# A list scheduler in place of a hand-written order, in a two-layer recurrent attention kernel on one core

## The chip, the cores and the metric

One core of a Trainium2 chip runs the whole program in one launch. The metric is the device time of that launch in microseconds (us). Its engines run side by side (in before PE is busy for 77%, DVE for 43% and ACT for 34% of the span), and the program gives each of them its instructions in a fixed order: PE (TensorE) does matmuls and writes them to the memory PSUM, DVE (VectorE) and ACT (ScalarE) do everything on vectors and empty PSUM, POOL (GpSimd) does a few copies, SP issues DMA. The kernel before takes 2516.9 us, median of three runs between 2516.39 and 2517.16.

## The reference, cut to what matters

```python
def _A_ref(x, mem0, Wq, Wk, Wv, Wo, seg_len):      # H = 16 heads of 256, model width 448
    mem = mem0                                      # 8 memory rows
    for s in range(2048 // 32):                     # 64 segments of 32 rows
        h = concat([mem, x[:, s*32:(s+1)*32]])      # 40 rows
        q, k, v = h @ Wq, h @ Wk, h @ Wv            # per head
        p = softmax(where(mask, q @ k.T / 16, -1e9))
        o = (p @ v) @ Wo                            # summed over heads
        mem = o[:8]; outs.append(o[8:])             # memory rows go to the next segment
def _B_ref(x, W_gate, W_up, W_down):                # width 1792
    return (relu(x @ W_gate) * (x @ W_up)) @ W_down
x = A_x
x = x + _A_ref(layernorm(x), ...);  x = x + _B_ref(layernorm(x), ...)
x = x + _A_ref(layernorm(x), ...);  x = x + _B_ref(layernorm(x), ...)   # same weights
```

The memory rows make a recurrence: segment s+1 cannot start before the memory rows of segment s are there. All else of a segment (its 32 ordinary rows, the output product, layer norm, the B layer) may come later.

## The kernel before

Set-up computes M = Wq·Wkᵀ and N = Wv·Wo for each head, so that scores are h·M·hᵀ and the output is P·h·N. After it the kernel makes 68 steps. Step t works on segment t of the first pair of layers and on segment t-4 of the second (`LAG = 4`), so steps 4 to 63 hold two segments and the four at each end hold one. Names used below:

- T: h·M, 7 units of 32 matmuls into one of two pairs of PSUM banks (`R<-hT,Mw` in the profile), each emptied by a copy to TTm (memory queries) and one to TTs (segment queries).
- The memory recurrence: scores from TTm (`bC<-hT,TTm`), softmax, transpose, P·h (`bC<-PTm,hK`), memory U·N (`bC<-Nw,UTm`), and back into hT through `selm`.
- Segment work: scores (`bG<-hT,TTs`), softmax, transpose (`bG<-ident,Ps`), segment products P·h in four quarters (`R<-PTs,hK`), copied to the buffer U.
- Once per pair of steps: U·N, 56 matmuls (`bO<-Nw,big`), layer norm with a transpose (`bG<-ident,xn`), gate and up (`R<-xBT,big`), down (`bO<-big,hB`), and the layer norm for the pair after next.

In the hand order, work that may wait stands in a list `fill`, from which every step takes bites with fixed sizes at fixed places.

```python
    def step(self, t):
        ...
        for i, k in enumerate([6, 0, 1, 2, 3, 4, 5]):
            S.t_unit(t, k, i % 2, ("act", "dve")[i % 2])      # bank pair and engine fixed
            for _ in range(2):
                if side: side.pop(0)()                        # ln_b, segment softmax of t-1
        ...
        useg = S.u_seg_units(t - 1)
        if s == 0: S.fill = useg + (S.un_units(p - 1) if p >= 1 else [])
        else:      S.fill = S.b_units(p - 1) if p >= 1 else []; late = useg
        S.run_fill(500);  S.s_mem(t); S.s_seg(t); S.run_fill(1500)
        S.p_t_mem(t); S.run_fill(400); S.u_mem(t)
        S.seg_mask(t)                                         # scores + mask, on DVE
        ...
    def un_units(self, p):
        uk = [("U", s, l, c) for s in range(2) for l in range(2) for c in range(4)]
        for k in range(0, NO, 2):                             # each waits for all of U
            def fn(k=k):
                sc.pe([MM(S.bO[:, 0:D], S.U[:, o, :], S.N[:, o, :], ...) for o in (k, k + 1)], uk, S.ps(4))
                ...
```

A helper turns each list of keys that an operation reads and writes into semaphore waits. Layer norm uses Ln and then Exp on ACT.

## Time and profile before

The first fence shows the page of the profile of before: span, busy time of each engine, the granted PE clock in 40 slices (9 is nine tenths or more), and the chain of waits by engine.

```profile
span 2520.5 us, 67762 instructions
...
PE 1940.4 (77%) x30924; PEld 1399.6 (56%) x30924; DVE 1074.5 (43%) x2630; ACT 861.8 (34%) x1859; POOL 94.3 (4%) x160
...
PEclk9778888898898888988898889888988888889888
...
PE 59%; DVE 24%; ACT 13%; issue 4%; POOL 0%; DVEq 0%; ACTq 0%; POOLq 0%
...
```

No engine is full. The second fence is the windows view of before for four stages: set-up, the single-layer steps at the head, steps 4 to 63, and the tail. After each stretch and its length come busy times and counts by engine, the clock, DMA share and rate. I set the borders at the first T matmul of steps 0, 4 and 64, which is found by counting (224 T matmuls a step).

```profile
...
core 0: us, PE busy (x) PEld busy (x) DVE busy (x) ACT busy (x) POOL busy (x), PEclk, DMA share, GB/s
0.00:110.70 110.70, 71.90 (x644) 48.03 (x644) 71.72 (x156) 63.56 (x126) 17.38 (x21) 0.89 0.61 179
110.70:214.70 104.00, 81.11 (x1484) 55.62 (x1485) 41.54 (x125) 25.44 (x70) 7.97 (x15) 0.80 0.01 3
214.70:2366.30 2151.60, 1665.94 (x26995) 1213.75 (x26995) 916.57 (x2219) 725.76 (x1556) 66.69 (x120) 0.88 0.01 3
2366.30:2520.50 154.20, 121.47 (x1802) 82.23 (x1802) 44.67 (x130) 47.05 (x109) 2.22 (x4) 0.85 0.01 3
...
```

Steps 4 to 63 take 2151.6 us, 71.72 us for each of 30 pairs of steps. PE is idle for 2151.60 - 1665.94 = 485.7 us of it, 16.2 us per pair, and its mean clock there is 0.88. In this trace the recorded clock is only ever 1.0 or 0.5, so that mean is (1 - 0.8847) · 2 = 23% of the time, 16.5 us per pair, at half clock (called cold below, and full clock warm; 0.8847 is the mean before rounding).

PE's part of the view of waits: who waited for whom, us in total, times, the longest.

```profile
...
engine line waited for: us in total, times, longest us
PE bG L126 <- DVE xn L507: 193.8, 35, 5.7
PE R L126 <- DVE big L294: 97.7, 40, 3.4
PE bG L126 <- DVE Ps L659: 77.0, 67, 1.7
PE bO L126 <- DVE big L294: 61.2, 32, 1.9
...
```

And the timeline of before, in three of the worst places of a pair: start, duration, engine, operation, and in brackets the idle time before it and what ended it.

```profile
...
start us, us, engine line op out<-in xcount [idle before <-releaser]
...
1002.32 0.39 PE L126 MATMUL R<-PTs,hK 40*128 40x512 bf16 x2 [3.06 <-DVE big L294]
...
1019.14 0.62 PE L126 MATMUL R<-PTs,hK 40*128 40x512 bf16 x6
...
1021.68 2.42 PE L126 MATMUL bO<-Nw,big 128*128 128x448 bf16 x6 [1.92 <-DVE big L294]
...
1040.93 1.28 ACT L498 ACT_TABLE_LOAD   x1
...
1042.23 0.29 ACT L498 ACTIVATE stat<-stat,cvec 128x1 f32<-128x1 f32 x1
1042.54 1.28 ACT L500 ACT_TABLE_LOAD   x1
...
1044.81 0.61 PE L126 MATMUL bG<-ident,xn 128*128 128x128 bf16 x4 [5.73 <-DVE xn L507]
...
```

A segment product (`R<-PTs,hK`) waits 3.06 us until the copies (`big<-R`) give back its bank pair. U·N (`bO<-Nw,big`) starts 1.92 us late because it waits for the last copy of the segment products. The transposes of the second layer norm wait 5.73 us, 2.56 us of which are two loads of ACT's function tables, one for Ln and one for Exp.

### The profile page before, as it was taken

To read this page: it belongs to the slowest core of one execution; us is meant where nothing else is said; L and a number is where in the kernel's file an instruction comes from. 1 tells how busy PE (TensorE), PEld (TensorE's weight loads), DVE (VectorE), ACT (ScalarE), POOL (GpSimd) and SP (SyncE) were. 2 spreads that over 40 slices of the span, in tenths; PEclk is the share of its full clock that TensorE was granted. 3 is DMA by queue.
4 is the path that set the end of the run, shared out by engine and by line. 5 is a ranking of instruction groups with operands and counts; after the bars stand their busy time and mean duration, and the time that the engine had idled before them with its cause. 6 is when DMAs were issued, how large, how long until landed. Compare 5 with 4: busy or idle time off the path is not lost.

```text
span 2520.5 us, 67762 instructions
## 1 busy us (share of the span) xinstructions
PE 1940.4 (77%) x30924; PEld 1399.6 (56%) x30924; DVE 1074.5 (43%) x2630; ACT 861.8 (34%) x1859; POOL 94.3 (4%) x160
## 2 busy tenths in 40 slices
PE   8578777787778777777787777777877777778787
PEld 5345555555555555555565555655555556555554
DVE  8334444344444444444444444444444443444332
ACT  7322333333333333333333333333333333333332
POOL 1100000000000000000000000000000000000000
PEclk9778888898898888988898889888988888889888
DMA  7300000000000000000000000000000000000000
GB/s 205 111 3 3 2 4 4 4 3 4 3 4 3 4 4 4 3 3 3 4 3 3 4 3 4 3 4 4 3 4 3 4 4 3 3 3 3 3 3 3
DMA packets 22302, 27.53 MB, mean 11 GB/s; under 512 B 5744, under 2 KB 15744, under 8 KB 22016
## 3 DMA queue, kind: packets, MB, share of 16 engines
q1 hardware_dynamic: 22016, 23.20, 3.2%
q8 instruction: 243, 3.98, 0.7%
q14 instruction: 43, 0.35, 0.0%
HBM read 21.35 MB, written 1.84 MB: 9 GB/s over the span
## 4 chain that ended last, share of the span: by engine, by line
PE 59%; DVE 24%; ACT 13%; issue 4%; POOL 0%; DVEq 0%; ACTq 0%; POOLq 0%
PE R L126 28%; PE bO L126 21%; PE bC L126 6%; DVE big L294 5%; DVE TTs L294 4%; ACT L500 3%; PE bG L126 3%; ACT TTs L292 2%; ACT L498 2%; DVE xn L507 2%; DVE TTm L294 1%; DVE hK L294 1%; DVE hB L800 1%; DVE stat L657 1%; DVE Ps L659 1%
## 5 line engine op out<-in xcount | busy, mean ns | idle before, releaser
L126 PE MATMUL R<-hT,Mw 128*128 128x80 bf16 (+1 forms) x15232 | 653.5, 212 | 45.2 <-issue 23.1
L126 PEld LDWEIGHTS R<-hT,Mw 128*128 128x128 bf16 x15232 | 639.3, 108 | 76.2 <-issue 38.6
L126 PE MATMUL bO<-Nw,big 128*128 128x448 bf16 x1904 | 437.9, 386 | 62.5 <-DVE big L294 61.2
L126 PEld LDWEIGHTS bO<-Nw,big 128*128 128x128 bf16 x1904 | 188.0, 105 | 260.7 <-DVE big L294 67.2
L292 ACT ACTIVATE TTm<-R 128x128 bf16<-128x128 f32 (+3 forms) x272 | 73.2, 269 | 634.2 <-PE R L126 609.8
L126 PE MATMUL R<-xBT,big 128*128 128x128 bf16 x3808 | 232.7, 220 | 28.2 <-ACT TTs L292 27.5
L126 PEld LDWEIGHTS R<-xBT,big 128*128 128x128 bf16 x3808 | 215.9, 98 | 33.9 <-ACT TTs L292 31.8
L294 DVE CAST TTm<-R 128x128 bf16<-128x128 f32 (+3 forms) x272 | 75.5, 277 | 308.9 <-PE R L126 283.8
L126 PE MATMUL R<-PTs,hK 40*128 40x512 bf16 (+1 forms) x640 | 95.3, 385 | 131.4 <-DVE big L294 97.7
L126 PE MATMUL bC<-Nw,UTm 128*32 128x448 bf16 x3752 | 194.6, 359 | 1.4 <-DVE UTm L294 1.4
L126 PE MATMUL bG<-ident,xn 128*128 128x128 bf16 x272 | 39.4, 297 | 193.8 <-DVE xn L507 193.8
L294 DVE CAST TTs<-R 128x512 bf16<-128x512 f32 (+3 forms) x272 | 177.0, 651 | 0.0
L294 DVE CAST big<-R 128x512 bf16<-128x512 f32 (+1 forms) x256 | 146.9, 618 | 53.7 <-PE R L126 50.8
L292 ACT ACTIVATE big<-R 128x512 bf16<-128x512 f32 (+2 forms) x268 | 136.2, 560 | 82.9 <-PE R L126 82.9
L294 POOL COPY hK<-xn 32x448 bf16<-32x448 bf16 x136 | 75.6, 556 | 2242.0 <-DVE xn L507 2235.6
L713 DVE TENSOR_TENSOR lo<-bC,hi 128x448 bf16<-128x448 f32 x67 | 41.9, 625 | 263.7 <-ACT hi L712 258.2
L800 DVE TENSOR_TENSOR hB<-gT,R 128x512 bf16<-128x512 bf16 (+1 forms) x136 | 84.2, 619 | 163.2 <-PE R L126 159.0
L292 ACT ACTIVATE TTs<-R 128x512 bf16<-128x512 f32 (+3 forms) x272 | 153.2, 563 | 0.0
L126 PEld LDWEIGHTS bC<-Nw,UTm 128*32 128x32 bf16 x3752 | 95.6, 98 | 94.8 <-issue 29.2
L126 PEld LDWEIGHTS bG<-ident,xn 128*128 128x128 bf16 x272 | 22.7, 126 | 209.1 <-DVE xn L507 209.1
L126 PEld LDWEIGHTS R<-PTs,hK 40*128 40x128 bf16 (+1 forms) x640 | 23.6, 101 | 189.7 <-DVE big L294 128.6
L126 PE MATMUL bO<-big,hB 128*128 128x448 bf16 x476 | 95.9, 353 | 21.0 <-DVE hB L800 21.0
(125 smaller groups left out, 1797.2 us busy)
## 6 DMA issues: line engine op xcount, KB each, us to landing
big<-in_A_Wo_dram SPq DMA_DIRECT2D x4, 896.0 KB, 6.0
big<-in_A_Wq_dram SPq DMA_DIRECT2D x4, 768.0 KB, 7.8
big<-in_A_Wk_dram SPq DMA_DIRECT2D x4, 768.0 KB, 9.2
big<-in_A_Wv_dram SPq DMA_DIRECT2D x4, 768.0 KB, 5.6
XA<-in_A_x_dram SPq DMA_DIRECT2D x32, 56.0 KB, 2.1
out_dram<-ys SPq DMA_DIRECT2D x32, 56.0 KB, 1.9
big<-in_B_W_down_dram SPq DMA_DIRECT2D x1, 1568.0 KB, 15.5
big<-in_B_W_gate_dram SPq DMA_DIRECT2D x1, 1344.0 KB, 6.9
```

What stands on the lines that cost most here:

```text
L126: ins = E.matmul(out, lhsT=lhsT, rhs=rhs, **kw)
L292: self.sc.op("act", lambda E: E.activation(out, src, ACT.Copy), reads, writes)
L294: self.sc.op(eng, lambda E: E.tensor_copy(out, src), reads, writes)
L498: sc.op("act", lambda E: E.activation(st[:, so + 8:so + 9], st[:, so + 7:so + 8], ACT.Ln, bias=S.cvec[:, 0:1], scale=1.0), [(key, 1), ("cv ...
L500: sc.op("act", lambda E: E.activation(st[:, so + 9:so + 10], st[:, so + 8:so + 9], ACT.Exp, scale=-0.5), [(key, 2)], [(key, 3)])
L507: sc.op("dve", lambda E, a=a, b=b, src=src: E.tensor_scalar(S.xn[:, i, a:b], src, st[:, so + 6:so + 7], st[:, so + 9:so + 10], op0=ALU.sub ...
L657: lambda: sc.op("dve", lambda E: E.tensor_reduce(st[:, 48:48 + n], Sm, AX.X, ALU.add), [("Sm",)], [("ss", 1)]),
L659: lambda: sc.op("dve", lambda E: E.tensor_tensor(dst, Sm, bc(56), ALU.mult), [("Sm",), ("ss", 2)], [("Ps",)]),
L713: sc.op("dve", lambda E: E.tensor_tensor(S.lo[:, :], b[:, 0:D], S.hi[:, :], ALU.subtract), S.ps(6) + [("hi",)], [("lo",)])
L800: sc.op("dve", lambda E: E.tensor_tensor(S.hB[:, 4 * k:4 * k + len(fcs), :].rearrange("p a b -> p (a b)"), S.gT[:, r, 0:n], S.banks[2 * r ...
```

## The change

The change intends to let a program find the order. Every operation past the set-up becomes a node with modelled durations, the keys it reads and writes, and one or two engines that may do it. A list scheduler then repeatedly takes, among operations that could start at about the same time, the one with the longest path behind it (the longest chain of operations that still has to follow); it also picks the PSUM bank pair and, for PSUM copies, ACT or DVE. The result is still a fixed program.

```diff
+    def graph(self):
+        ...
+        for o in reversed(self.ops):
+            own = min(o.cost.values()) + self.LAT[o.eng[0]]
+            o.prio = own + max([q.prio + 60.0 for q in o.succs], default=0.0)
+    def run(self):
+        while len(order) < total:
+            for e in self.ENGS:
+                ...                                     # start time of each ready candidate on e
+                lim = max(f, t0) + (60.0 if e == "pe" else 40.0)
+                t, o = max((x for x in lst if x[0] <= lim), key=lambda x: (x[1].prio, -x[0]))
+            ...
+            if len(o.eng) > 1:                          # the engine that ends first takes a copy
+                ...
@@ scalar engine
+                    eng.add_instruction(mybir.InstLoadActFuncSet(act_func_set_id=LN_EXP, name="I-4000000"))
@@ s_seg: the mask is added by PE
+            out = [MM(b[:, 0:8 * KEYS], S.ident[:, :], S.maskr[:, :], start=True, stop=False)]
@@ un
-            def fn(k=k):
-                sc.pe([MM(S.bO[:, 0:D], S.U[:, o, :], ...) for o in (k, k + 1)], uk, S.ps(4))
+            S.mm(lambda k=k: [MM(S.bO[:, 0:D], S.U[:, o, :], ...) for o in (k, k + 1)],
+                 2 * S.pitch(D), uk, S.ps(4))           # uk as before: all of U
@@ b_layer: seven pieces instead of four, down waits piece by piece
-        for k in range(4):
+        for k in range(7):
+            fcs = (2 * k, 2 * k + 1)
+            R = S.tile("R", 2)
@@ _need: DVE and ACT also wait for their own earlier readers of what they overwrite
-                if src != eng or eng == "pool":
+                if src != eng or eng != "pe":
@@ step: no fill, no places
-        S.run_fill(500)
-        ...
+        S.s_seg(t); S.seg_pt(t); S.u_seg(t)
+        if s == 1:
+            ...
+            S.un(p); S.ln_b(p); S.b_layer(p)
+            if p + 2 < NP: S.ln_a(p + 2)
```

(Cut to its core; cuts are marked with dots.)

## The prediction

> **What bounds it now.** Three stages, seen in the windows view: set-up until the first matmul of the recurrence at 110.7 us; eight single-layer steps at the ends (104 us before 214.7, 92 us after 2428.9); between them 60 two-layer steps, 2214 us, or 73.8 us per pair of steps. The pairs decide. In a pair PE is busy 57 us, DVE 31, ACT 24.5: no engine is full; the order of the PE stream is the limit. The timeline of one pair shows PE still for 5.7 us before the transposes of the second layer norm (bG<-ident,xn), 3.1 and 1.9 us around the copies of the segment products (big<-R), and about 1 us several times around softmax and TTs copies. The chain of waits agrees: PE 59%, DVE 24%, ACT 13%.
>
> The idle stretches cost twice. [...] after the 5.7 us gap the granted clock reads 0.50, and elsewhere 32 cold T matmuls (R<-hT,Mw) take 2.3 us where warm ones take 1.3. The mean clock of a pair is 0.88.
>
> **What PE needs, from stretches with clock 1.00 (estimate).** Per pair: T 448 at 36 ns (96 in 3.60 us) 16.1; U·N 56 at 189 ns (24 in 4.70) 10.6; memory U·N twice 2.83, 5.7; gate/up 112 at 56 ns, 6.3; down 2.7; small products and transposes about 8; array-shape switches and the added mask matmul about 1.3. Together about 51 of 73.8 us.
>
> **What the change does.** Arithmetic is nearly the same. It removes the mask add on DVE (0.48 us, twice a pair; a 320-wide matmul replaces it) and the ACT table loads (136 of 1.28 us; two before each layer norm, 2.6 us of its latency). Gate/up goes in 7 pieces instead of 4 (about +0.9 us of ACT and DVE per pair). Above all it moves: U·N, the B layer and layer norms leave their fixed slots, T units may run ahead, copies choose the engine that ends first.
>
> Two loops could prevent filling. The memory recurrence: T 8.1 us, copies, softmax and transposes about 6.5, memory U·N 2.8: about 18 us per step, 36 per pair, below 51. The other, scores, U·N, layer norm, B, layer norm, to T of the pair after next, is about 35 us by its durations and has over one pair of time. So PE should bind, with leftovers where both loops wait or copies hold the two R bank pairs: I allow 4 us.
>
> **Sum.** Set-up 110; 30 pairs at 54.5, 1635; head about 85, tail about 83. About **1915 us**, 8 in 10 between **1835 and 2030**. Faster by over 2%: 0.97; within: 0.02; slower: 0.01.
>
> **What would show it.** PE busy 88 to 93% of the span, no idle over 3 us in the pairs; clock 0.97 or more; pairs of 53 to 57 us; no ACT_TABLE_LOAD past the start; "PE bG <- DVE xn" waits (194 us) almost gone; chain mainly PE. Set-up still ends at 110.
>
> **What would make it wrong.** The static order rests on modelled times; engines run in order, so one late copy stalls PE: then many waits of 0.3 to 1 us and 58 to 62 us per pair. Finer alternation of shapes could cost PE more. If the greedy order finishes the filler early, the recurrence is left alone with 5 us idle per step. [...]

110 + 1635 + 85 + 83 is 1913, about 1915 us. The smaller terms are estimates, and these measured numbers stand behind them. At full clock in before, a memory U·N matmul starts 283 ns after a U·N matmul and not 189 (33 places), so a change of array shape costs about 94 ns there; with 17 changes a pair that would make 1.6 us, more than the 1.3 estimated. The mask matmul took 136 ns (after, start to start). A copy of 512 columns took 597 ns on ACT and 688 on DVE for the gate and up products, one of 256 columns 383 and 412, which gives the 0.9 us for seven pieces. And that one late copy stalls PE is seen in before: `lo`, which the next `selm` matmuls read, was ready at 1001.15 us, but they started at 1003.15, behind the segment product that stood still for a bank until 1002.32.

## The result, and the profile after

The kernel after takes 1988.25 us (median of four fast runs, 1986.36 to 1989.57) against 2517.03 for before in the same rounds. The ratio is 0.7898, 95% interval 0.7884 to 0.7911. Here and below a ratio is the mean time of one kernel's fast runs over that of before's fast runs of the same rounds, so it is not quite the ratio of the medians quoted. The forecast was 1915 us, with a range of 1835 to 2030: the result lies in the range, 73 us above the middle.

The same lines of the page of after:

```profile
span 1986.3 us, 68251 instructions
...
PE 1825.2 (92%) x30992; PEld 1305.1 (66%) x30992; DVE 1013.9 (51%) x2529; ACT 771.0 (39%) x1960; POOL 94.3 (5%) x160
...
PEclk9869999999999999999999999999999999999999
...
PE 68%; DVE 17%; ACT 2%; issue 1%; DVEq 0%
...
```

The windows view of after for the same four stages, borders found in the same way:

```profile
...
0.00:111.30 111.30, 73.00 (x644) 49.22 (x645) 73.87 (x158) 61.79 (x127) 17.49 (x21) 0.90 0.59 178
111.30:205.10 93.80, 84.32 (x1528) 56.42 (x1529) 31.70 (x110) 29.21 (x87) 7.95 (x15) 0.87 0.01 3
205.10:1870.10 1665.00, 1564.56 (x27071) 1127.68 (x27070) 867.54 (x2132) 644.60 (x1646) 66.68 (x120) 0.96 0.02 4
1870.10:1986.30 116.20, 103.29 (x1753) 71.78 (x1752) 40.80 (x129) 35.35 (x100) 2.22 (x4) 0.94 0.01 4
...
```

A pair of steps takes 1665.0 / 30 = 55.50 us. PE idle fell from 16.2 to (1665.00 - 1564.56) / 30 = 3.35 us per pair, cold time from 16.5 to 4.2. So 12.8 of the 16.2 us that a pair lost are idle time. The rest is for the most part PE work done at a better clock: from one T matmul to the next it now takes 36.3 ns on the average where it took 42.1 (442 such distances in a pair before: 2.6 us).

PE's waits in after (total us, times, longest):

```profile
...
PE R L127 <- DVE big L710: 47.4, 61, 1.4
PE bO L127 <- DVE big L710: 25.2, 31, 0.8
...
PE bG L127 <- DVE xn L743: 7.0, 4, 3.7
...
```

The wait of 193.8 us for the layer norm has gone. What is left is for the most part one place (2.4 of the 3.35 us idle per pair), shown by the timeline of after:

```profile
...
966.86 1.96 DVE L710 CAST big<-R 128x512 bf16<-128x512 f32 x3
...
967.70 0.39 PE L127 MATMUL R<-PTs,hK 40*128 40x512 bf16 x2 [1.38 <-DVE big L710]
...
968.74 0.23 DVE L826 TENSOR_REDUCE stat<-bC 128x2 f32<-128x80 f32 x1
...
969.45 3.14 PE L127 MATMUL bO<-Nw,big 128*128 128x448 bf16 x8 [0.84 <-DVE big L710]
...
```

The segment products (`R<-PTs,hK`) of the second step of a pair stand still 1.38 us for a bank pair, then U·N 0.84 us for the last copy. DVE works without a pause here (`big<-R`, three copies in 1.96 us), and the memory softmax, which would give PE other work, begins behind those copies (968.74). The windows view of after, one microsecond each, with the clock as the third number from the end:

```profile
...
966.00:967.00 1.00, 0.32 (x4) 0.00 (x0) 0.94 (x3) 0.85 (x2) 0.00 (x0) 1.00 0.00 0
967.00:968.00 1.00, 0.30 (x2) 0.12 (x2) 1.00 (x2) 0.23 (x1) 0.00 (x0) 1.00 0.00 0
968.00:969.00 1.00, 0.40 (x6) 0.14 (x4) 1.00 (x4) 0.87 (x2) 0.00 (x0) 1.00 0.24 57
969.00:970.00 1.00, 0.55 (x2) 0.28 (x3) 0.97 (x3) 0.30 (x2) 0.00 (x0) 0.73 0.00 0
970.00:971.00 1.00, 1.00 (x4) 0.40 (x3) 0.76 (x6) 0.50 (x2) 0.00 (x0) 0.50 0.00 0
...
973.00:974.00 1.00, 1.00 (x15) 0.41 (x13) 0.00 (x0) 0.01 (x1) 0.73 (x2) 1.00 0.00 0
...
```

Just after that place the clock halves, with no single idle gap above 1.38 us: PE was busy for 0.30 to 0.55 us of each microsecond. The first 8 matmuls of U·N then take 3.14 us, about twice their warm time (1.69 us for 8 in before, at 1031.12 us). The whole trace shows the same: all changes of the clock lie on a grid of 3.413 us, and in steps 4 to 63 PE was busy for 29 to 53% of the 30 full-clock stretches of this grid after which the clock halved, and for 74 to 100% of the 418 after which it stayed full. In before the two ranges overlap (0 to 65%, and 49 to 100%), so the busy share alone does not settle it.

### The profile page after: what moved, and what is told of

It is laid out like the page before. It is cut to its first block, busy times and chain, and to the rows that moved or that the text cites. A ratio compares the mean times of both kernels' runs of the same rounds, so it can differ in the third digit from the quotient of the medians.

```text
span 1986.3 us, 68251 instructions
## 1 busy us (share of the span) xinstructions
PE 1825.2 (92%) x30992; PEld 1305.1 (66%) x30992; DVE 1013.9 (51%) x2529; ACT 771.0 (39%) x1960; POOL 94.3 (5%) x160
## 4 chain that ended last, share of the span: by engine, by line
PE 68%; DVE 17%; ACT 2%; issue 1%; DVEq 0%
PE R L127 35%; PE bO L127 22%; PE bC L127 8%; DVE big L710 7%; PE bG L127 2%; DVE stat L736 1%; DVE ys L1007 1%; DVE xn L743 1%; DVE XA L1003 1%; DVE hK L710 1%; DVE UTm L710 1%; DVE XB L978 1%; DVE Ps L870 1%; DVE hB L996 1%; DVE stat L868 1%
## 5 line engine op out<-in xcount | busy, mean ns | idle before, releaser
L127 PE MATMUL R<-hT,Mw 128*128 128x80 bf16 (+1 forms) x15232 | 548.7, 200 | 23.9 <-POOL hT L710 22.9
L127 PEld LDWEIGHTS R<-hT,Mw 128*128 128x128 bf16 x15232 | 539.7, 100 | 39.0 <-issue 24.0
L127 PE MATMUL bO<-Nw,big 128*128 128x448 bf16 x1904 | 463.5, 388 | 25.2 <-DVE big L710 25.2
L127 PE MATMUL R<-xBT,big 128*128 128x128 bf16 x3808 | 251.7, 220 | 22.9 <-DVE xBT L710 22.2
L996 DVE TENSOR_TENSOR hB<-gT,R 128x256 bf16<-128x256 bf16 x238 | 100.0, 420 | 325.4 <-ACT gT L995 322.4
L127 PEld LDWEIGHTS R<-xBT,big 128*128 128x128 bf16 x3808 | 224.6, 98 | 46.2 <-DVE xBT L710 27.7
L995 ACT ACTIVATE gT<-R 128x256 bf16<-128x256 f32 x238 | 91.2, 383 | 183.4 <-PE R L127 179.5
L709 ACT ACTIVATE big<-R 128x512 bf16<-128x512 f32 (+1 forms) x263 | 134.6, 543 | 63.3 <-PE R L127 61.9
L710 DVE CAST big<-R 128x512 bf16<-128x512 f32 (+1 forms) x249 | 148.7, 619 | 14.6 <-PE R L127 12.5
L709 ACT ACTIVATE hK<-bC 8x448 bf16<-8x448 f32 x96 | 51.4, 535 | 202.1 <-PE bC L127 200.5
L127 PE MATMUL bO<-big,hB 128*128 128x448 bf16 x476 | 129.2, 354 | 0.0
```

What stands on the lines that cost most here:

```text
L127: ins = E.matmul(out, lhsT=lhsT, rhs=rhs, **kw)
L709: return E.activation(out(), src(), ACT.Copy)
L710: return E.tensor_copy(out(), src())
L995: S.act(lambda E, k=k, R=R: E.activation(S.gT[:, k % 2, 0:256], R.b(0)[:, 0:256], ACT.Relu), 256, R.res(0), [("gT", k % 2)])
L996: S.dve(lambda E, k=k, R=R: E.tensor_tensor(S.hB[:, 2 * k:2 * k + 2, :].rearrange("p a b -> p (a b)"), S.gT[:, k % 2, 0:256], R.b(1)[:, 0: ...
```

## The experiments

All twelve kernels of the experiments gave correct results. The indented passages below are the expectations before each run was built (U·N is written U.N there). "Pair" is the mean time of a pair in steps 4 to 63 of the profiled run, idle and cold are per pair and found as above (in b_tables, whose full clock is recorded as 0.949, cold is the time at 0.5).

| run | median us | ratio to before | pair us | PE idle us | cold us |
|---|---|---|---|---|---|
| before | 2517.0 | 1 | 71.72 | 16.2 | 16.5 |
| after | 1988.3 | 0.7898 | 55.50 | 3.35 | 4.2 |
| b_tables | 2399.4 | 0.9541 | 68.90 | 12.9 | 11.8 |
| b_warm | 2480.1 | 0.9840 | 70.58 | 9.9 | 5.7 |
| b_warm2 | 2402.7 | 0.9541 | 68.07 | 8.1 | 2.5 |
| b_allbut | 2320.5 | 0.9217 | 65.77 | 10.9 | 11.3 |
| b_uk | 2215.7 | 0.8797 | 62.53 | 9.1 | 7.9 |
| a_tables_back | 2077.4 | 0.8238 | 58.09 | 4.8 | 6.9 |
| a_fixed | 2002.0 | 0.7951 | 55.82 | 3.6 | 4.6 |
| a_prog | 2277.8 | 0.9049 | 64.30 | 7.2 | 13.2 |
| a_flat | 2211.5 | 0.8778 | 62.70 | 6.3 | 14.0 |
| a_nolat | 1928.3 | 0.7652 | 53.78 | 2.8 | 0.1 |
| a_uk | 1868.3 | 0.7412 | 51.79 | 1.5 | 0.0 |
| a_uk_flat | 2014.3 | 0.7995 | 56.32 | 4.5 | 1.7 |

Runs that begin with b_ start from the kernel before, those with a_ from the kernel after. Where two kernels of different rounds are compared, I divide their ratios to before. In b_warm and b_warm2 dummy matmuls count as busy.

### How much is not the order: the table set alone

My theory was that the order pays; the first rival was that the table loads, which the change also removes, carry most of it.

```diff
 # b_tables: before, plus
+                    eng.add_instruction(mybir.InstLoadActFuncSet(act_func_set_id=6, name="I-4000000"))
 # a_tables_back: after, minus
-                    eng.add_instruction(mybir.InstLoadActFuncSet(act_func_set_id=LN_EXP, name="I-4000000"))
```

> The kernel before, with one ACT table set loaded at the start and nothing else. Theory O (the order is what pays): of the 5.7 us idle before the second layer norm's transposes 2.6 us are the two table loads, so a pair of steps falls from 71.7 to about 68 us (2.6 idle and about 1 of cold clock); the first layer norm's loads are off the path. Total 2390 to 2430 us. Rival T (the removed loads carry most of the gain of the change): total under 2250 us.

> The kernel after, same order, without the one table set, so that the 136 table loads are back. Theory O: the order covers layer norm latency with other PE work, so a pair grows by 1 to 2.5 us from 55.5, total 2020 to 2065. Rival T (the removed loads carry the gain): a pair grows by 5 us or more, total over 2140.

b_tables came out at 2399.4 us, ratio 0.9541, inside what theory O expected. (Its profiled run was 2425.3 us against 2397.1 to 2399.6 for the other three. Its trace records a clock of 0.949 wherever the other traces record 1.0, so its row in the table is a little long. Without this run the ratio would be 0.951.) Removing the loads in the hand order is worth 4.6 points (4.9 without that run) of the 21.0 that the change gained. Putting them back under the new order costs 0.8238 / 0.7898 = 1.043, 4.3%, and 2.6 us a pair. That is more than the 1 to 2.5 us expected: the new order, made without knowing of the loads, covers them hardly better than the hand order (89 us against 118). Neither run comes near the rival's numbers.

One load serves both Ln and Exp here: before has 137 loads of 1.28 us each, after has one, at its start, and its layer norms and softmaxes run behind it.

### Everything but the order

b_allbut puts the other parts of the change on the hand order, except that some keys of after are finer (half banks for the copies of memory rows and the residual sums); those count with the order here. The first two operations of the segment softmax then read PSUM directly, where the mask add stood.

```diff
 # b_allbut: before, with the table set, and
-            sc.op("dve", lambda E: E.tensor_tensor(S.Sm[:, :, :], S.bG[...], mk8, ALU.add), ...)
+        mms = [MM(S.bG[:, 0:8 * KEYS], S.ident[:, :], S.maskr[:, :], start=True, stop=False)]
-        for k in range(4):          # gate/up
+        for k in range(7):
-                      [("hB", i) for i in range(4)] + [("Wd",)], S.ps(4))
+                      [("hB", k // 2)] + [("Wd",)], S.ps(4))
-                if src != eng or eng == "pool":
+                if src != eng or eng != "pe":
```

> Everything of the change but the order, on the hand order of before: one table set, the mask added by a PE matmul, gate/up in seven pieces with the down product waiting piece by piece, own-engine waits. Theory O (the order pays the most): about what the table set gives alone, 66 to 69 us a pair, total 2330 to 2420, so that the new order with its choice of engines is worth 350 us or more. Rival R (these other edits together make most of the gain): under 2200 us.

It takes 2320.5 us, ratio 0.9217. That is 9.5 us below what theory O expected in total and 0.2 us in a pair, and leaves 332 us to the order, not 350 or more; theory O stands with a smaller share. So 7.8 of the 21.0 points are not the order: 4.6 for the table set, 3.2 for the rest together (4.9 and 3.0 without the slow run of b_tables). The other 13.2 points, the 332 us between 2320.5 and 1988.3, belong to the new order with its choice of banks and engines, and to the finer keys. (The finer keys alone can hardly be much of it: a_prog below has them too, with a worse order, and ends up only 2% below b_allbut.) How the 3.2 points divide among the mask, the seven pieces and the finer wait of the down product was not separated by a run. The waits fit the first and the last: PE's wait for the segment softmax (`bG` for `DVE Ps`) falls from 2.3 to 1.1 us a pair between b_tables and b_allbut, and the 0.6 us before the down product disappears.

### What idle time costs a second time

The prediction said that idle PE stretches cost twice, through the clock. Dummy matmuls test that: they do no useful work, so anything that they win, the clock wins.

```diff
 # b_warm: before, plus (results overwritten later)
+    def dummies(self, bank, n):
+        S.sc.pe([MM(S.banks[bank][:, 0:D], S.N[:, 0, 0:128], S.N[:, 1, :], start=True, stop=True) for _ in range(n)], (), S.ps(bank))
+        S.dummies(5, 24)                 # before the transposes of the second layer norm
+                if c == 2 and s == 1:    # before a segment product;  b_warm2: s == 0
+                    S.dummies(4, 12)
+                if k == 0:
+                    S.dummies(4, 8)      # before U.N
```

> The kernel before, with 24, 12 and 8 dummy matmuls of 448 columns put into its three longest PE idle stretches of a pair (results overwritten). They add no useful work and should delay nothing. Theory C (idle costs a second time through the clock): cold time per pair falls from 16.5 us to under 6, T matmuls come every 37 ns instead of 42, a pair falls from 71.7 to 66 to 68 us, total about 2350 to 2400. Rival (the clock is off the path, the waits behind it take up the gain): within 1% of 2517, or slower by the dummies.

> As b_warm, with the 12 dummies moved: in b_warm they stood in the step whose segment products are not followed by the 3.1 us wait, so that wait kept its cold clock after it (5.7 us per pair) and the dummies pushed the U.N there back by 1.8 us. Theory C: cold time per pair under 2 us, T every 36 to 37 ns, a pair 67 to 68.5 us, total 2375 to 2415. Rival (the clock is off the path): no better than b_warm's 2480.

b_warm missed its numbers (2480.1 us), because of a mistake of mine: the twelve dummies stood in the wrong step of the pair, left the 3.1 us wait as it was and pushed U·N back in the other step. Moved in b_warm2 they gave 2402.7 us, a gain of 4.6%, and 68.07 us a pair. The windows view of b_warm2 for steps 4 to 63:

```profile
...
208.50:2250.60 2042.10, 1799.63 (x28315) 1259.50 (x28315) 912.07 (x2219) 728.27 (x1556) 66.98 (x120) 0.98 0.01 4
...
```

The clock is 0.98 there instead of 0.88. From one T matmul to the next it took 38.1 ns instead of 42.1, and from one U·N matmul to the next 189.7 instead of 213.9; with 442 and 51 such distances in a pair these make 1.8 and 1.2 of the 3.65 us that a pair lost. The expectation was met in total and pair, but not quite in clock: cold time is 2.5 us and not under 2, and T comes every 38.1 ns and not every 36 to 37. Of the 16.2 us per pair that the change gains, at least 3.65 could thus be had by keeping the clock up in the old order.

### What in the scheduler pays

Three runs take one part of it away each.

```diff
 # a_fixed: every PSUM copy on the engine that it had before, for example
-                 nm, R.res(), [("TTm", k)])
+                 nm, R.res(), [("TTm", k)], eng=(("act", "dve")[(k + 1) % 2],))
 # a_prog: after the longest paths are computed
+        for n, o in enumerate(self.ops):
+            o.prio = -float(n)
 # a_flat: in add()
+        o.cost = {e: 500.0 for e in o.cost}
```

> The kernel after, scheduled anew with every PSUM copy nailed to the engine that it had before. Theory E (the free choice matters, since TTm and TTs of one bank then go to two engines at once and R is free sooner): 1 to 3 us more a pair, total 2020 to 2080. Rival: the scheduler orders around it, within 1% of 1988.

> The kernel after, with program order in place of the longest path as the priority among operations that can start. Theory L (the longest-path priority is what makes the fill good): over 58 us a pair, total over 2060. Rival G (free choice among what is ready is enough, whatever the priority): within 1.5% of 1988.

> The kernel after, ordered with every operation modelled at 500 ns, latencies between engines kept. Theory M (the order is only as good as its durations): 1 to 4 us more a pair, total 2020 to 2110. Rival G (graph and priority are enough, since semaphores correct the rest): within 1% of 1988.

The free choice of engine is worth little: a_fixed is at 0.7951 / 0.7898 = 1.007. That theory fell, the rival was right. The priority is worth much: with program order as the priority, a_prog takes 2277.8 us, 14.6% more than after, and only 2% less than b_allbut, which has the hand order. The timeline of a_prog shows why (PE only):

```profile
...
1041.42 10.76 PE L127 MATMUL bO<-Nw,big 128*128 128x448 bf16 x56
...
1070.91 0.31 PE L127 MATMUL bG<-maskr,ident 128*128 128x320 bf16 x1 [0.75 <-ACT hT L711]
...
1072.71 0.52 PE L127 MATMUL bC<-PTm,hK 40*128 40x128 bf16 x10 [0.37 <-ACT PTm L711]
1074.06 5.42 PE L127 MATMUL bC<-Nw,UTm 128*32 128x448 bf16 x56 [0.83 <-ACT UTm L711]
...
```

U·N is spent in one run of 10.8 us as soon as it can go. Later, from 1070 us on, the memory recurrence stands alone, and each of its stages makes PE wait for a copy or a softmax. No gap is as long as 1 us, yet the clock falls; the memory U·N takes 5.42 us where a warm one takes 2.83. The windows view of a_prog for the same place shows the clock:

```profile
...
1070.00:1075.00 5.00, 2.95 (x59) 1.81 (x60) 3.70 (x10) 1.99 (x6) 1.78 (x4) 0.81 0.00 0
1075.00:1080.00 5.00, 5.00 (x52) 1.98 (x44) 0.06 (x1) 0.47 (x1) 0.00 (x0) 0.51 0.01 3
...
```

With the longest path as priority, U·N and the B layer are dealt out in pieces of two to sixteen matmuls between the stages of the recurrence, as far as they last.

The durations matter as well: a_flat, ordered as if each operation took 500 ns, takes 2211.5 us, 11.1% more than after. The loss of 223 us is nearly twice the most that I had expected. PE's waits in a_flat:

```profile
...
PE bC L127 <- DVE Pm L833: 78.2, 63, 2.1
...
```

The largest is one for the memory softmax (`Pm`), 78.2 us in all. The timeline shows operations of a layer norm and of the segment softmax between those of the memory softmax in DVE's fixed order. After has 0.9 us of that wait. Its cold time is 14.0 us a pair, near that of the kernel before. Flat durations change the priorities, the start times that the scheduler reckons with and its choice of engines all at once; no run separates these, and only the choice of engines is known to be worth little (a_fixed).

### The wait that is left

The place found in after (2.4 us of idle per pair, then cold clock) has two waits: 1.56 us per pair in which the segment products wait for a bank pair, and 0.80 in which U·N waits for the last copies. U·N cannot fill the first one because it is declared to wait for all of U: so in before, and the change kept the line. Each U·N matmul reads one block of U, which one quarter of the segment products writes.

```diff
 # a_uk: after, with
-        uk = [("U", s, l, c) for s in range(2) for l in range(2) for c in range(4)]
         for k in range(0, NO, 2):
+            uk = [("U", s, l, k // 16) for s in range(2) for l in range(2)]
 # b_uk: the same in b_allbut, and by hand
-                S.fill = useg + (S.un_units(p - 1) if p >= 1 else [])
+                S.fill = useg[:2] + un[:8] + useg[2:3] + un[8:16] + useg[3:] + un[16:]
```

> The kernel after, with each U.N matmul pair made to depend on the four copies of its own quarter of U instead of all eight or sixteen; the scheduler orders anew. Theory W (what is left, 3.35 us idle and 4.2 us of cold clock per pair, comes from U.N waiting for the last copies of the segment products): idle at those places falls from 2.6 to under 0.8 us per pair, cold time to under 1, a pair from 55.5 to about 52, total about 1880. Rival P (PE is at its limit or the R banks bind): within 1% of 1988.

> Everything but the order on the hand order (b_allbut, 2320), with U.N depending on its own quarter of U and its matmuls put between the segment products by hand. Theory W (U.N held back by the last copy is a fault of the declared dependence, in either order): the 1.8 us wait before U.N and most of the 2.2 us wait before the third segment product go, with the cold clock after them; a pair from 65.8 to 62 to 64 us, total 2200 to 2270. Rival (the hand order's other waits take it up): within 1% of 2320.

a_uk takes 1868.3 us, ratio 0.7412: 6.2% less than after (0.7412 / 0.7898 = 0.938), 25.9% less than before. It beats both and computes the same. Its timeline (PE only) shows what went:

```profile
...
1015.82 0.61 PE L127 MATMUL R<-PTs,hK 40*128 40x512 bf16 x4
...
1017.39 2.82 PE L127 MATMUL bO<-Nw,big 128*128 128x448 bf16 x14 [0.64 <-ACT big L709]
...
1026.46 0.39 PE L127 MATMUL R<-PTs,hK 40*128 40x512 bf16 x2
...
```

U·N itself still waits, 0.62 us per pair instead of 0.80. But a quarter of it now stands, with the memory U·N behind it, between the segment products and covers their copies, and the 1.56 us for the bank pair are gone. The windows view of a_uk for steps 4 to 63:

```profile
...
199.30:1752.80 1553.50, 1509.14 (x27071) 1120.35 (x27071) 863.36 (x2101) 654.63 (x1679) 67.03 (x120) 1.00 0.02 5
...
```

The clock is full throughout, and PE idle is (1553.50 - 1509.14) / 30 = 1.48 us per pair. PE needs 1509.14 / 30 = 50.3 us per pair, so little is left for a better order of this work. As the scheduler orders everything anew, not all of the 6.2% need come from this one line (a_nolat below gains 3.1% by another order of the same work); in the hand order, where only U·N is moved, the test is cleaner.

In the hand order the same edit gives 0.8797 / 0.9217 = 0.954, a pair of 62.53 us, within what was expected. One step of that expectation was wrong: only the wait of U·N went. PE's waits in b_uk:

```profile
...
PE R L127 <- DVE big L296: 69.0, 64, 2.0
...
```

The wait of U·N (57.3 us in b_allbut) is no longer in the view. The wait of the third segment product for its bank pair is still there (69.0 us, 69.1 in b_allbut), since it stands in the other step of the pair, where no U·N is at hand. The gain came through U·N and the clock behind it.

### A model without latencies, and flat durations on the better graph

```diff
 # a_nolat: after, with
-    LAT = {"pe": 170.0, "act": 0.0, "dve": 0.0, "pool": 60.0, "sp": 2200.0}
+    LAT = {"pe": 0.0, "act": 0.0, "dve": 0.0, "pool": 0.0, "sp": 0.0}
-        return 90.0 if b == "pe" else 35.0
+        return 0.0
 # a_uk_flat: a_uk, with the line of a_flat
```

> The kernel after, ordered with right durations but with no latency of results and no hop between engines. Theory M: the model then thinks that a result is ready 0.1 to 0.3 us too early and puts its user ahead of work that could go, so PE gains many short waits: 0.5 to 2 us more a pair, total 2005 to 2050. Rival G: within 0.5% of 1988.

> a_uk with every operation modelled at 500 ns, as in a_flat. Theory M: with PE near its limit a wrong order shows more, 1 to 4 us more a pair than a_uk's 51.8, total 1900 to 1990. Rival G: within 1% of 1868.

The 0.1 to 0.3 us of the first expectation are the latencies of the model. Of such delays before shows these: PE started 57 ns after the end of the DVE instruction that it waited for (`Ps`, 67 times), ACT 34 ns after DVE (`Em`, 66), DVE 32 ns after ACT (`Fm`, 67), and DVE began its copy of the memory transpose 0.27 to 0.35 us after that matmul had started (35 times).

a_uk_flat lost a little more than theory M expected: 4.5 us a pair, 2014.3 us, 0.7995 / 0.7412 = 1.079. a_nolat missed altogether, and so did its rival: 1928.3 us, 3.1% faster than after. The worse model (it also takes DMA's latency for nothing, which is 2.1 us from issue to landing for the loads of `XA` in after) gave the better order. PE idle hardly changed (2.8 against 3.35 us a pair), but no gap exceeds 1 us and the cold time is gone (0.1 us). The timeline of a_nolat at the place where after stands still:

```profile
...
1047.99 0.60 PE L127 MATMUL R<-PTs,hK 40*128 40x512 bf16 x4
1048.52 2.83 PE L127 MATMUL bC<-Nw,UTm 128*32 128x448 bf16 x56
1051.29 0.62 PE L127 MATMUL R<-PTs,hK 40*128 40x512 bf16 x6
...
```

Here the memory U·N, 2.83 us of work that needs nothing from the segment products, happens to stand between two of them, so that their copies are covered. In after it starts at 974.86 us, 7 us after the segment product that waits at 967.70. I take this for chance: nothing in the model aims at it. But no run shows that, and with one run of the kind it stays open whether latencies in the model help or hurt in general. What the run does show is that a greedy order of this graph can be several per cent off for reasons that have nothing to do with the truth of its model.

## Why the prediction was right

The range held the result and the mechanism was the stated one. Stage by stage, against the sum of the prediction:

| stage | predicted us | measured us | error us |
|---|---|---|---|
| set-up | 110 | 111.3 | 1 |
| head, steps 0 to 3 | 85 | 93.8 | 9 |
| 30 pairs | 1635 (54.5 each) | 1665.0 (55.50 each) | 30 |
| tail | 83 | 116.2 | 33 |

- **The tail was mis-sized by a wrong border.** The prediction put the end of the two-layer steps at 2428.9 us. That is the start of step 66, not of step 64. Step 64 starts at 2366.3 us; so a pair took 71.72 us before and not 73.8, and the tail was 154.2 us and not 92. So the stretch that the sum took for 30 pairs held 31, and the sum left one pair of single-layer steps out: in after steps 64 and 65 take 50.3 us. What the prediction called the tail, from step 66 on, came out at 65.9 us and not 83, so a second error of 17 us hid part of the first. The tail as a whole is the largest term of the miss, and one count of the steps would have shown the border wrong.
- **"What PE needs … about 51."** Right. a_uk, with hardly any idle time and full clock, shows 50.3 us of busy PE per pair.
- **"I allow 4 us" of leftovers.** The size was close (55.50 - 51 = 4.5), the reason only in part. I named both loops waiting and the two bank pairs held by copies. Both are there: of the 3.35 us idle 1.56 are segment products waiting for a bank pair, and 0.69 are gate and up waiting for xBT while the memory rows are still being copied. The rest of the 4.5 is for the most part U·N's own wait (0.80) and the cold clock (PE is busy for 52.15 us in after and 50.3 in a_uk), which the allowance did not name; nor did it name the fault of the graph that kept U·N from filling the gap: it waited for all of U. a_uk is 3.7 us a pair shorter. I had seen the wait in the profile of before and read it as a matter of order.
- **"Clock 0.97 or more."** Wrong: 0.96 in the pairs and 0.95 over the profiled run. I took only gaps of over 3 us as harmful, which was an estimate and is not what the traces show. There was none over 3 us in the pairs, as predicted, and not even one over 1.4, and 4.2 us per pair were still cold.
- **"Idle stretches cost twice."** Right: b_warm2 wins 4.6% with work that is thrown away.
- **The other signs** held: PE busy 92%, pairs within 53 to 57 us, one table load, the `PE bG <- DVE xn` wait down from 193.8 to 7.0 us, chain mainly PE (68%), mean duration of a T matmul down from 215 to 202 ns, set-up until 111 us.
- **Table loads and mask.** Costed rightly as latency, but I gave no share. Together with the pieces and finer waits they are 7.8 of 21.0 points.
- **"What would make it wrong."** The case named there, a recurrence left alone with about 5 us idle per step after the filler is spent, did not happen in after. a_prog shows it in kind: 7.2 us idle a pair and 13.2 us cold, which makes 64.30 us a pair.
- **The head** shrank by 10 us instead of 19. No run looked into it.

## What to carry to other kernels

When no engine is full, add up what the busiest engine needs at full speed, and look for the order that gets there; a list scheduler with a longest-path priority and modelled durations near the measured ones won 13 points here where the same scheduler with program order as its priority won hardly anything over the hand order. Then look at what still waits, and ask whether the graph declares more than the data need: one line of dependence was worth 6% after all the reordering, and 4.6% in the hand order. Judge gaps by how thin PE's work is over a few microseconds and not by the longest of them (in after the clock halved where PE was busy for 29 to 53% of 3.413 us, with no gap above 1.4 us), and count the stages before dividing a span by them.
